# Delta-rule attention with a gated convolution behind it: the state kept as its block diagonal

## The chip, the cores and the metric

One core of a Trainium2 chip runs the kernel. The time is the device time in microseconds of one execution, from the launch of the program to its end; the smaller it is, the better. Beside it stands one execution taken by the hardware profiler, whose span runs from the first instruction to the last.

## What is computed

Four batches of eight heads, 768 tokens, 40 values a head. A state of 40 x 40 per batch and head is carried over the tokens; then 320 values a token go through a gated layer with a convolution over three tokens.

```python
for t in range(S):
    y[:, :, t] = einsum('bhd,bhde->bhe', r_t, state)
    Sa = einsum('bhde,bhe->bhd', state, a_t)
    state = state * w_t[:, :, None, :] - einsum('bhd,bhe->bhde', Sa, b_t)
    state = state + einsum('bhd,bhe->bhde', v_t, k_t)
x = y.transpose(0, 2, 1, 3).reshape(B, S, H * D)        # 4 x 768 x 320
h = maximum(x @ w_in, 0)                                 # 320 -> 1024
gate = sigmoid(conv over t of h with conv_w, three taps)
out = (h * gate) @ w_out                                 # 1024 -> 320
```

The weights of the second part come as 64-bit floats, all else as 32-bit floats.

## The kernel before

**Tiling.** The tokens are cut into 24 steps of 32. The four batches stand beside one another, 32 tokens each, on 128 partitions (`quad(bi)` is the batch's quarter). Two steps make a pair j for loading and solving, and also a window of 64 tokens for the second part. Heads are taken in three groups g of 120 values (three heads), at columns `GC = (0, 120, 200)`, so the third group overlaps the second by one head.

**The parts of a step** (two letters each in the written order):

- `ld` loads w, a, k, b of a pair; `lr` and `lv` load r and v of a step, one transfer a batch. `de` makes the products of w before and behind each token (`pre`, `suf`) with VectorE scans, and `wc`, the decay over a whole step, one column for each head with zeros elsewhere. `dd` turns a, k, b on TensorE and multiplies by these products (`ah`, `kt`, `bt`).
- `sc` makes three masked copies of `ah` (`ap`, ScalarE) and with them the 32 x 32 scores `at`; `si` and `so` solve the triangular system of a pair on VectorE (even j) or GpSimd (odd j), with the scores sent through DRAM before and the result after. `ha` turns k and b back to `khat`, `bhat`, with tokens on partitions.
- `ch` is the recurrence, in four parts. First `pp` = a times the old state (line 514) plus the scores times v (522), copied to `psb` by ScalarE. Then `pu` = solve times `psb` (533), copied to `u`. Then `pn` = khat times v plus bhat times u (549): for every batch and group a full 120 x 120 block, of which the three 40 x 40 blocks on the diagonal are the states. VectorE adds `pn` to the old state (562), 120 x 360 for each batch. Last, GpSimd multiplies by `wc` (568), which also clears what lies off the diagonal.
- `rt`, `vt`, `ut` turn r, v, u; r also in three masked copies `rp` (579) beside the plain one `rt` (584). `st` turns the state, three transposes and one ScalarE copy `sn` for each batch (602, 604). `pa` and `ou` make the step's result `py` from the turned state (629) and the masked pairs (638); `fi` turns and scales it into `xf` and splits it into a rounded part `xh` and the rest `xl`.
- `pk` packs with three transfers the rows that the second part's last passes need; `mi` does x @ w_in (eight passes, line 700), the convolution, the sigmoid and the gate for two of eight column blocks; `mo` the product with w_out (754) and the store. `we` converts the 64-bit weights piece by piece on VectorE, ScalarE and GpSimd.

**Order.** Every part is a generator that yields between its stages. The string `ORDER` lists the parts one stage at a time, as all engines are to be given their instructions; `put` names what each stage needs done ahead of it, and `advance` runs that first where the order hasn't. Each engine works through its own list in that order; all transfers go through SP's queue. PSUM has eight banks: six for the attention (`bank`), two for the second part. `BUFS` gives the number of buffers of each name.

## Time and profile before

| | |
|---|---|
| median of three timed runs | 707.8 us (705.96 to 711.5) |
| the profiled execution, first to last instruction | 704.2 us |
| around the span, against the median of the runs | 3.6 us |
| mean granted TensorE clock | 0.903 |
| instructions | 29851 |
| TensorE matmul / weight load busy | 559.1 / 496.7 us |
| VectorE, ScalarE, GpSimd busy | 521.5, 360.5, 354.1 us |
| DMA | 53.40 MB in 242402 packets, 229000 of them under 512 B |

How to read it: PE is TensorE's matmul, PEld its weight load, which runs beside the matmuls; DVE is VectorE, ACT ScalarE, POOL GpSimd, SP the engine that issues the transfers. In a row for a group of instructions, `pn<-v,khat 32*120 32x120` means that `pn` is written from `v` and `khat`, with 32 rows and 120 columns of weights, and 32 partitions of 120 elements moving through; `xcount` is the number of records, then come busy time, mean ns of one, and the idle time of the engine before them with what ended it. The busy time of a group counts overlapping instructions once. A row of a timeline gives start, length, engine, line and instruction. The ends of matmuls are modelled, so the distance from one start to the next is the safer measure.

### The profile page before, as it was taken

The numbers are of one execution on the slowest core, as the hardware profiler recorded it, in microseconds if no ns is written. First come the engines' busy times: TensorE is split into PE (matmuls) and PEld (weight loads), VectorE is DVE, ScalarE is ACT, GpSimd is POOL, SyncE is SP. The second block draws the span as 40 slices with busy tenths as digits, with TensorE's granted clock in tenths as the row PEclk, the third lists the DMA queues.
The fourth block names the chain that finished last, engine by engine and source line by source line (L and its number), as shares of the span: only waits on it lengthen the run. The fifth ranks groups of instructions, "written<-read, shape, count | busy, mean of one in ns | idle before, by whom it ended". The sixth has DMA issues, their size and how long they took to land. (4 is left out here: it accounts for less than half of the span.)

```text
span 704.2 us, 29851 instructions
## 1 busy us (share of the span) xinstructions
PE 559.1 (79%) x13021; PEld 496.7 (71%) x13021; DVE 521.5 (74%) x1169; ACT 360.5 (51%) x884; POOL 354.1 (50%) x582
## 2 busy tenths in 40 slices
PE   4436765678688987988987996899998977899886
PEld 3335654666577876977867885788887876788775
DVE  6699789998988895558884478986869892446561
ACT  3322344354275455655464664477665545566661
POOL 2002884037785236783244883237976048854321
PEclk9756766897899998999999998999999999999998
DMA  8766456348036325444414356524444025021000
GB/s 139 121 117 117 96 111 103 86 103 159 7 61 107 61 49 90 87 78 81 84 29 90 75 95 101 81 61 68 86 69 87 11 65 84 20 50 32 22 29 19
DMA packets 242402, 53.40 MB, mean 76 GB/s; under 512 B 229000, under 2 KB 238112, under 8 KB 242272
## 3 DMA queue, kind: packets, MB, share of 16 engines
q1 hardware_dynamic: 242272, 51.50, 40.2%
q8 instruction: 102, 1.67, 1.0%
q14 instruction: 28, 0.23, 0.1%
HBM read 38.63 MB, written 10.22 MB: 69 GB/s over the span
## 5 line engine op out<-in xcount | busy, mean ns | idle before, releaser
L729 DVE SCALAR_TENSOR_TENSOR cc<-hb,cw,cc 128x256 f32<-128x256 f32 x192 | 107.0, 580 | 28.6 <-ACT cc L721 25.0
L568 POOL TENSOR_TENSOR s<-s,wc 120x360 f32<-120x360 f32 x88 | 75.2, 885 | 66.6 <-DVE s L562 66.6
L480 POOL TENSOR_TENSOR st<-xx,bb 128x126 f32<-128x126 f32 (+22 forms) x186 | 81.0, 436 | 20.8 <-DMA bb<-bd 8.1
L486 POOL TENSOR_TENSOR xx<-xx,st 128x126 f32<-128x126 f32 (+22 forms) x186 | 81.8, 440 | 14.6
L700 PE MATMUL ph<-xh,wih 120*128 120x256 f32 x288 | 56.2, 304 | 12.0 <-ACT hb L714 12.0
L562 DVE TENSOR_TENSOR s<-pn,s 120x360 f32<-120x360 f32 x88 | 40.6, 523 | 28.7 <-PE pn L549 28.7
L736 DVE TENSOR_TENSOR cc<-cc,hb 128x512 f32<-128x512 f32 x48 | 40.9, 859 | 26.2 <-ACT cc L734 26.1
L480 DVE TENSOR_TENSOR st<-xx,bb 128x126 f32<-128x126 f32 (+22 forms) x186 | 53.7, 289 | 7.5 <-DMA bb<-bd 1.7
L486 DVE TENSOR_TENSOR xx<-xx,st 128x126 f32<-128x126 f32 (+22 forms) x186 | 54.4, 292 | 6.4
L700 PEld LDWEIGHTS ph<-xh,wih 120*128 120x128 f32 x288 | 41.4, 193 | 17.0 <-ACT hb L714 13.8
L734 ACT ACTIVATE cc<-cc 128x512 f32<-128x512 f32 x48 | 30.5, 637 | 40.8 <-DVE cc L729 40.8
L667 POOL TENSOR_TENSOR xl<-xf,xh 120x384 fp32r<-120x384 f32 x24 | 26.3, 1095 | 44.8 <-ACT xh L665 44.8
L721 ACT ACTIVATE cc<-hb,cw 128x256 f32<-128x256 f32 x96 | 43.8, 507 | 5.0 <-POOL g21l L743 2.4
L427 ACT ACTIVATE ap<-ah,hmask 120x384 f32<-120x384 f32 (+1 forms) x72 | 36.6, 577 | 18.3 <-DVE ah L391 9.7
L604 ACT COPY sn<-pt 120x360 f32<-120x360 f32 x92 | 39.0, 470 | 10.9 <-PE pt L602 10.4
L602 PE MATMUL pt<-ident,s 120*120 120x120 f32 x276 | 40.7, 281 | 4.0 <-DVE s L562 2.4
L714 ACT ACTIVATE hb<-ph 128x512 f32<-128x512 f32 x48 | 28.8, 601 | 22.3 <-PE ph L700 20.5
L579 ACT ACTIVATE rp<-pr,hmask 120x384 f32<-120x384 f32 x72 | 36.7, 585 | 4.7 <-PE pr L576 4.3
L700 PE MATMUL ph<-xl,wih 120*128 120x256 f32 x192 | 39.0, 285 | 0.0
L533 PE MATMUL pu<-psb,tt 32*32 32x40 f32 x1536 | 22.4, 210 | 18.8 <-ACT psb L527 16.1
L602 PEld LDWEIGHTS pt<-ident,s 120*120 120x120 f32 x276 | 31.6, 144 | 6.1 <-DVE s L562 2.8
L533 PEld LDWEIGHTS pu<-psb,tt 32*32 32x32 f32 x1536 | 18.6, 115 | 23.6 <-ACT psb L527 18.1
(867 smaller groups left out, 1661.8 us busy)
## 6 DMA issues: line engine op xcount, KB each, us to landing
bb<-bd SPq DMA_DIRECT2D x24, 256.0 KB
w<-in_w_dram SPq DMA_DIRECT2D x24, 160.0 KB
a<-in_a_dram SPq DMA_DIRECT2D x24, 160.0 KB
k<-in_k_dram SPq DMA_DIRECT2D x24, 160.0 KB
b<-in_b_dram SPq DMA_DIRECT2D x24, 160.0 KB
r<-in_r_dram SPq DMA_DIRECT2D x96, 40.0 KB
v<-in_v_dram SPq DMA_DIRECT2D x96, 40.0 KB
out_dram<-ob SPq DMA_DIRECT2D x22, 160.0 KB
```

Source lines behind the costliest of these rows:

```text
L480: eng.tensor_tensor(t3, xx[:, 0:nj, i : i + 1].to_broadcast([128, nj, nt]), bb[:, i : i + 1, i + 1 :].to_broadcast([128, nj, nt]), ALU.mult,)
L486: eng.tensor_tensor(xx[:, 0:nj, i + 1 :], xx[:, 0:nj, i + 1 :], t3, ALU.add)
L533: nc.tensor.matmul(pu[quad(bi), hc], tt[quad(bi), c, h, :], psb[quad(bi), hc], start=(h == 0), stop=True, skip_group_check=True,)
L562: nc.vector.tensor_tensor(new, pn[bi][:GR], old[bi], ALU.add)
L568: nc.gpsimd.tensor_tensor(n4, n4, w4, ALU.mult)
L579: nc.scalar.activation(out=rp[:, :, h, :], in_=pr[:GR], func=AF.Copy, scale=hmask[:, h : h + 1])
L602: nc.tensor.transpose(pt[:GR, g, :], old[bi][:, g, :], ident[:GR, :GR])
L604: nc.scalar.copy(sn, pt[:GR])
L700: nc.tensor.matmul(ph[:, j], l[:, fs], x, start=(j == 0 and i == 0), stop=(i == len(passes) - 1), skip_group_check=True,)
L721: nc.scalar.activation(out=cc[:, j], in_=hb[:, j, :, 1 : W + 1], func=AF.Copy, scale=cw[:, 1, f : f + 1],)
L729: nc.vector.scalar_tensor_tensor(out=cc[:, j], in0=hb[:, j, :, x : W + x], scalar=cw[:, x, f : f + 1], in1=cc[:, j], op0=ALU.mult, op1=ALU ...
L736: nc.vector.tensor_tensor(cc, cc, hb[:, :, :, 1 : W + 1], ALU.mult)
```

## The change

The state of a step becomes one tile of 120 x 480: for each batch and group the 120 rows (three heads of 40) and only 40 columns, that is the three diagonal blocks on top of one another. To write that form, `khat` and `bhat` are kept in 840 columns, each head's 40 among zeros (`slots`, `spot`), so that a window of 120 columns holds one head and zeros for the two others; `pn` then takes 32 products of 40 columns a side, which add up in place. `pp` and `py` read the state head by head, with the masked copies `ap` and `rp` as weights; the plain `rt` goes. `st` turns all four batches with four transposes and one copy. The decay `wc` needs no zeros any more and is written by the product that made `al`. GpSimd scales the state of all batches in one instruction.

The groups become (3, 3, 2) heads without overlap. r and v are stored by head number modulo three (`at(q)` gives a head's place), which needs the heads in another order: `reorder` copies r and v in four blocks of steps (`CUT`) from DRAM to DRAM, 24 transfers a block, and a step's load is then one transfer. Tiles that are read past their last head get a constant pad once (`padded`). In the second part, the pack is two transfers into `xh` and `xl` themselves in place of `xp`, and the passes are ordered anew. Buffers and needs follow. The order string is another one throughout. Cut to its core:

```diff
-    ld=4, r=2, v=2, hat=2, suf=2, pre=3, al=2, wc=3, at=3, ah=3, kt=2, ap=1, rp=1, bb=1, xx=1, stmp=1,
-    tt=2, rt=1, s=2, psb=1, u=2, vt=2, sn=4, ms=1, ysb=1, xf=2, xh=2, xl=2, xp=1, hb=2, cc=2, o=2,
+    r=2, v=2, hat=3, suf=2, pre=3, wc=3, at=3, ah=2, kt=2, ap=3, rp=1, bb=1, xx=1, stmp=1,
+    tt=2, s=2, psb=1, u=2, vt=2, sn=1, ms=1, xf=1, xh=2, xl=2, hb=2, cc=2, o=2,
...
-    ld0 de0.0*2 ld0*2 de0.1 ld0 ld1 de0.1 we0 dd0.0*3 dd0.1*2 sc0 dd0.1 we0 ld1*2 lr0 sc0 sc1 lr1
...
+    ld0*2 de0.0*2 de0.1*2 dd0.0 ld0 dd0.0 ld0 dd0.0 dd0.1 ld0 de0.0 de0.1 dd0.0 dd0.1*2 sc0 we0 we1
+    ld1 ha0 de1.0 ld1 we0*2 sc0 sc1 ha0 ha1 de1.0 ha0 de1.1 re0 ld1 we0 ha1 we0 we2 ld1 dd1.0 sc1
+    si0 sc1 ha1 we1 we2 dd0.1 ld1 we2 dd1.0 we1 re0 dd1.0 de1.1 re0 dd1.1*2 de1.1 re0 sc2 de1.0 lv0
+    lv1 dd1.1 so0*2 we2 so0 ld2 so0 we1 ha2 lv0 de2.0 vt0 so0*2 we3 lr0 so0*2 si0 we3 we4 sc2 ld2
+    we3*2 we5 de2.0 so0 we3 ch0 lr1 sc2 sc3 so0 rt0 sc3 lr0 so0 we4 so0 ch0 we4 we5 ch0*2 ut0 pa0
...
-GC = (0, 120, 200)
-GH = ((0, 3), (0, 3), (1, 3))
+NH = (3, 3, 2)
+CUT = (0, 2, 8, 16, 24)
+PG = 280
+PH = 120
...
+    def padded(name, at, value):
+        t = cp.tile([128, at + D], F32, name=name)
+        nc.gpsimd.memset(t[:, at:], value)
+        return t
+
+    inb = {nm: padded(f"in{nm}", 2 * HD, 1.0) for nm in "wakb"}
+    tok = {nm: [padded(f"{nm}{i}t", HD, 0.0) for i in range(BUFS[nm])] for nm in "rvu"}
+    ysb = padded("ysb", HD, 0.0)
+    hat = {}
+    for i in range(BUFS["hat"]):
+        for nm in "kb":
+            hat[nm, i] = cp.tile([128, G * PG], F32, name=f"hat{nm}{i}")
+            nc.vector.memset(hat[nm, i], 0.0)
...
-        nc.scalar.copy(wih[0:D, 2, :], wil[0:D, 2, :])
-        yield
-        nc.sync.dma_start(wil[2 * D : GR, 1, :].bitcast(F32), wil[D : 2 * D, 2, :].bitcast(F32))
-        nc.sync.dma_start(wil[0:D, 2, :].bitcast(F32), wil[2 * D : GR, 2, :].bitcast(F32))
-        nc.sync.dma_start(wil[D:GR, 2, :].bitcast(F32), wih[D:GR, 2, :].bitcast(F32))
+        for x, t in ((0, wih), (D, wil)):
+            nc.sync.dma_start(
+                t[2 * D : GR, 2, :].bitcast(F32), wil[x : x + D, 2, :].bitcast(F32)
+            )
+        yield
+        nc.scalar.copy(wil[0 : 2 * D, 2, :], wih[0 : 2 * D, 2, :].bitcast(F32))
...
+    def reorder(z):
+
+        t0, t1 = CUT[z] * C, CUT[z + 1] * C
+        for nm in "vr":
+            ordered[nm, z] = dc.tile([B, t1 - t0, HD], F32, name=f"{nm}o{z}")
         for bi in range(B):
-            nc.sync.dma_start(t[quad(bi)], x[bi, :, t0 : t0 + C, :].rearrange("h t d -> t h d"))
-        st[nm] = t.rearrange("p h d -> p (h d)")
+            for nm, x in (("v", v), ("r", r)):
+                for h in range(3):
+                    nc.sync.dma_start(
+                        ordered[nm, z][bi, :, 3 * h * D : (3 * h + NH[h]) * D].rearrange(
+                            "t (g d) -> t g d", d=D
+                        ),
+                        x[bi, h::3, t0:t1, :].rearrange("g t d -> t g d"),
+                    )
+            yield
+
+    def load(nm, st):
+        st[nm] = tok[nm][st["n"] % BUFS[nm]]
+        z = block(st["n"])
+        t0 = (st["n"] - CUT[z]) * C
+        nc.sync.dma_start(st[nm][:, :HD], ordered[nm, z][:, t0 : t0 + C, :])
...
-        al = buf(wn, [GR, NS, 1], "al", f"al{j}{y}")
-        nc.vector.tensor_tensor(al, suf[:, :, 0:1], wr[:, :, 1:2], ALU.mult)
-        nc.vector.reciprocal(dp0[:, :, 0:1], al)
+        al = pd["wc"].rearrange("p c (z y) g -> p y g z c", y=2)[:, y]
+        nc.vector.tensor_tensor(al, ends(suf, 0), ends(wr, 1), ALU.mult)
+        nc.vector.reciprocal(ends(dp0, 0), al)
         nc.vector.tensor_tensor_scan(
             out=flat(pd["pre"][:, y]), data0=flat(wr), data1=flat(dp0),
             initial=0.0, op0=ALU.mult, op1=ALU.add,
-        )
-        bc = [GR, 2 * G, 2, 3]
-        nc.vector.tensor_tensor(
-            pair(pd["wc"], y), al.rearrange("p (s c) x -> p s c x", c=2).to_broadcast(bc),
-            hmask.unsqueeze(1).unsqueeze(1).to_broadcast(bc), ALU.mult,
...
-            nc.scalar.copy(pd[nm][:, c], pz)
+            st[nm] = hat[nm, n % BUFS["hat"]]
+            nc.scalar.copy(
+                slots(st[nm]), pz.rearrange("p (g h d) -> p g h d", g=G, h=3)
+            )
             yield
 
+    def slots(t):
+
+        t = t.rearrange("p (g x) -> p g x", g=G)[:, :, : 2 * PH + D]
+        return bass.AP(tensor=t.tensor, offset=t.offset, ap=[*t.ap[:2], [PH, 3], [1, D]])
+
+    def spot(q):
+        return PG * (q // 3) + PH * (q % 3)
...
-            for g in range(G):
-                lo = GH[g][0] * D
+            for q, g, h in heads():
                 for bi in range(B):
                     nc.tensor.matmul(
-                        pp[quad(bi), GC[g] + lo : GC[g] + GR], ah[:, g, quad(bi)],
-                        old[bi][:, g, lo:],
-                        start=(g == 0), stop=False, skip_group_check=True,
+                        pp[quad(bi), q * D : (q + 1) * D], st["ap"][:, q, quad(bi)],
+                        old[:, bi, g],
...
-        for x, (l, m) in enumerate(((kk, vv), (bk, uu))):
-            for g in range(G):
+        pn = [bank([128, G, D], f"pn{n}{bi}") for bi in range(B)]
+        for x, (l, m) in enumerate(((st["k"], vv), (st["b"], uu))):
+            for q, g, h in heads():
+                lo = spot(q) - D * h
                 for bi in range(B):
                     nc.tensor.matmul(
-                        pn[bi][:GR, g, :], l[quad(bi), cols(g)], m[quad(bi), cols(g)],
-                        start=(x == 0 and g == 0), stop=(x == 1), skip_group_check=True,
+                        pn[bi][:GR, g, :], l[quad(bi), lo : lo + GR],
+                        m[quad(bi), at(q)],
+                        start=(x == 0 and q == 0), stop=(x == 1), skip_group_check=True,
                     )
+        new = state[n + 1] = buf(wn, [GR, B, G, D], "s", f"s{n}")
+        w4 = nxt["pd"]["wc"][:, nxt["c"]].unsqueeze(3).to_broadcast([GR, B, G, D])
         for bi in range(B):
-            new = wn.tile([GR, G, GR], F32, tag=f"s{bi}", bufs=BUFS["s"], name=f"s{n}{bi}")
-            n4 = new.rearrange("p g (h d) -> p g h d", h=3)
-            w4 = wc[:, :, bi, :].unsqueeze(3).to_broadcast([GR, G, 3, D])
             if first:
-                nc.vector.tensor_tensor(
-                    n4, pn[bi][:GR].rearrange("p g (h d) -> p g h d", h=3), w4, ALU.mult
-                )
+                nc.vector.tensor_tensor(new[:, bi], pn[bi][:GR], w4[:, bi], ALU.mult)
             else:
-                nc.vector.tensor_tensor(new, pn[bi][:GR], old[bi], ALU.add)
-            state[n + 1].append(new)
-            scaled.append((n4, w4))
+                nc.vector.tensor_tensor(new[:, bi], pn[bi][:GR], old[:, bi], ALU.add)
         yield
         if not first:
-            for n4, w4 in scaled:
-                nc.gpsimd.tensor_tensor(n4, n4, w4, ALU.mult)
-        yield
-
+            nc.gpsimd.tensor_tensor(new, new, w4, ALU.mult)
...
+    def at(q):
+
+        p = 3 * (q % 3) + q // 3
+        return slice(p * D, (p + 1) * D)
...
+        rp = st["rp"] = buf(wn, [GR, H, BC], "rp", f"rp{n}")
+        for g in range(G):
             nc.scalar.activation(
-                out=rp[:, :, h, :], in_=pr[:GR], func=AF.Copy, scale=hmask[:, h : h + 1]
-            )
-        if n:
-            st["rt"] = buf(wn, [GR, G, BC], "rt", f"rt{n}")
-            nc.scalar.copy(st["rt"], pr[:GR])
...
-        st["sn"] = []
+        pt = bank([128, B, GR], f"pt{n}")
         for bi in range(B):
-            pt = bank([128, G, GR], f"pt{n}{bi}")
-            for g in range(G):
-                nc.tensor.transpose(pt[:GR, g, :], old[bi][:, g, :], ident[:GR, :GR])
-            sn = buf(wn, [GR, G, GR], "sn", f"sn{n}{bi}")
-            nc.scalar.copy(sn, pt[:GR])
-            st["sn"].append(sn)
-            yield
+            nc.tensor.transpose(pt[:GR, bi, :], old[:, bi].rearrange("p g d -> p (g d)"), ident[:GR, :GR])
+        sn = st["sn"] = buf(wn, [GR, B, GR], "sn", f"sn{n}")
+        nc.scalar.copy(sn, pt[:GR])
...
-            for g in range(G):
-                lo = GH[g][0] * D
+            for q, g, h in heads():
                 for bi in range(B):
                     nc.tensor.matmul(
-                        py[quad(bi), GC[g] + lo : GC[g] + GR], st["rt"][:, g, quad(bi)],
-                        st["sn"][bi][:, g, lo:],
-                        start=(g == 0), stop=False, skip_group_check=True,
+                        py[quad(bi), q * D : (q + 1) * D], st["rp"][:, q, quad(bi)],
+                        st["sn"][:, bi, h * D : (h + 1) * D],
...
-        xp = wd["xp"] = buf(mo, [GR, B, W], "xp", f"xp{n}", F32R)
-        nc.sync.dma_start(xp[0 : 2 * D].bitcast(F32), xh[0 : 2 * D, 1].bitcast(F32))
-        nc.sync.dma_start(xp[2 * D : GR].bitcast(F32), xh[D : 2 * D, 2].bitcast(F32))
-        nc.sync.dma_start(xl[0:D, 2].bitcast(F32), xh[2 * D : GR, 2].bitcast(F32))
+        for x, t in ((0, xh), (D, xl)):
+            nc.sync.dma_start(t[2 * D : GR, 2].bitcast(F32), xh[x : x + D, 2].bitcast(F32))
...
-            (wil[:, 0], xh[:, 0]), (wih[:, 0], xl[:, 0]), (wih[:, 1], xl[:, 1]),
-            (wil[:, 1], xp), (wil[:, 2], xl[:, 2]),
+            (wil[:, 0], xh[:, 0]), (wil[:, 1], xh[:, 1]), (wih[:, 0], xl[:, 0]),
+            (wih[:, 1], xl[:, 1]), (wil[:, 2], xl[:, 2]),
...
-                (0, ("chain", 2 * (j - BUFS["ah"]) + 1), 1), (1, ("wakb", j), 3), (2, ("wakb", j), 4),
+                (0, ("scores", 2 * (j - BUFS["ah"]) + 1), 1), (1, ("wakb", j), 3), (2, ("wakb", j), 4),
...
+            (1, ("chain", 2 * (j - BUFS["at"]) + 1), 1), (0, ("chain", n - BUFS["ap"]), 1),
         )
         put(
             ("hats", n), lambda st=st: hats(st), (0, ("decayed", j, 1), 2), (1, ("decayed", j, 1), 3),
-            (0, ("hats", n - 1), 2), (0, ("outputs", 2 * (j - BUFS["hat"]) + 1), 1),
-            (0, ("chain", 2 * (j - BUFS["hat"]) + 1), 3),
-        )
-        put(
-            ("v", n), lambda st=st: load(v, "v", st), (0, ("v", n - 1), 1),
+            (0, ("hats", n - 1), 2), (0, ("outputs", n - BUFS["hat"]), 1),
+            (0, ("chain", n - BUFS["hat"]), 3),
...
+            ("v", n), lambda st=st: load("v", st), (0, ("reorder", block(n)), B), (0, ("v", n - 1), 1),
...
```

More of the change, by code (lines that the diff above doesn't have):

```diff
@@ L314, in cols, with heads @@
     def cols(g):
-        return slice(GC[g], GC[g] + GR)
+        return slice(g * GR, (g + 1) * GR)
+    def heads():
+        return ((q, q // 3, q % 3) for q in range(H))
     def load_wakb(pd):
@@ L576, in rturn @@
             nc.tensor.transpose(pr[:GR, g, :], st["r"][:, cols(g)], ident)
[L577 to L578 removed]
+        rp = st["rp"] = buf(wn, [GR, H, BC], "rp", f"rp{n}")
+        for g in range(G):
             nc.scalar.activation(
[L580 removed]
+                out=rp[:, by_rows(g)], in_=pr[:GR, : NH[g]], func=AF.Copy, scale=hmask[:, g : g + 1]
             )
[L582 to L584 removed]
         yield
@@ L654, in finish @@
         for g in range(G):
-            nc.tensor.transpose(pq[:GR, g, :], st["ysb"][:, cols(g)], ident)
+            nc.tensor.transpose(pq[:GR, g, :], ysb[:, cols(g)], ident)
         xf = buf(wn, [GR, G, B, C], "xf", f"xf{n}")
@@ L854, in tile_decay_delta_attention_then_conv_gate_moe @@
     )
+    for z in range(len(CUT) - 1):
+        put(("reorder", z), lambda z=z: reorder(z))
     for pd in pds:
@@ L899, in tile_decay_delta_attention_then_conv_gate_moe @@
         put(
-            ("r", n), lambda st=st: load(r, "r", st), (0, ("r", n - 1), 1),
+            ("r", n), lambda st=st: load("r", st), (0, ("reorder", block(n)), B), (0, ("r", n - 1), 1),
             (0, ("rturn", n - BUFS["r"]), 1),
```

253 lines of the change are left out of this document (139 added, 114 removed).

## The prediction

> **What bounds the kernel now.** I read the page's table of engines first, then the busy time in three stretches of the span (columns of the second: from and to, length, busy us and instructions of PE, PE's weight loads, DVE, ACT, POOL, then the granted clock, the DMA share and GB/s).
>
> ```profile
> span 704.2 us, 29851 instructions
> PE 559.1 (79%) x13021; PEld 496.7 (71%) x13021; DVE 521.5 (74%) x1169; ACT 360.5 (51%) x884; POOL 354.1 (50%) x582
> ```
> ```profile
> 0.00:200.00 200.00, 122.87 (x2921) 104.39 (x2921) 172.68 (x442) 74.30 (x176) 86.74 (x166) 0.77 0.54 102
> 200.00:650.00 450.00, 393.58 (x9503) 354.01 (x9501) 324.77 (x687) 259.57 (x643) 254.40 (x406) 0.96 0.40 71
> 650.00:704.30 54.30, 42.66 (x603) 38.31 (x601) 24.05 (x41) 26.62 (x66) 13.01 (x11) 0.94 0.07 23
> ```
>
> No engine bounds the whole. In the first 200 us VectorE is busy 172.7 us (86%), with the weight conversion and the first solves; TensorE has a clock of 0.77 there and much idle time. From 200 to 650 us TensorE is busy 393.6 of 450 us (87%) at a clock of 0.96, VectorE 72%. In the last 54 us TensorE leads alone. So the change has two prices: what it takes from VectorE counts early, what it does to TensorE counts after that. What is left of TensorE's idle time in the middle, 450 - 393.6 = 56.4 us, is made of waits, and I asked for them by releaser:
>
> ```profile
> engine line waited for: us in total, times, longest us
> PE ph L700 <- ACT hb L714: 11.2, 8, 5.4
> ...
> PE pu L533 <- ACT psb L527: 3.9, 5, 1.3
> PE pm L411 <- ACT rp L579: 3.9, 3, 3.3
> ...
> PE pn L549 <- ACT u L538: 2.6, 2, 1.6
> ```
>
> These four end with a ScalarE eviction and sum to 21.6 of the 56.4 us; the largest is the wait for hb, a copy out of a bank. No row of this answer waits for the state on GpSimd, so the recurrence itself is not what holds TensorE in this stretch.
>
> **The change on TensorE.** Three places issue other matmuls. Here are the blocks of one step, each to be read from its start to the start of the next row.
>
> ```profile
> 401.21 0.79 PE L533 MATMUL pu<-psb,tt 32*32 32x40 f32 x64
> 401.93 0.62 PE L700 MATMUL ph<-xh,wih 120*128 120x256 f32 x3
> ...
> 403.08 0.90 PE L549 MATMUL pn<-v,khat 32*120 32x120 f32 x24
> 403.80 0.81 PE L549 MATMUL pn<-u,bhat 32*120 32x120 f32 x24
> 404.54 0.53 PE L450 MATMUL pz15b<-ident,bt 120*128 120x120 f32 x3
> ...
> 410.24 1.67 PE L602 MATMUL pt<-ident,s 120*120 120x120 f32 x12 [1.59 <-ACT wx L366]
> 411.85 0.65 PE L411 MATMUL pm<-rp,vt 120*32 120x96 f32 x24
> ...
> 428.50 0.76 PE L514 MATMUL pp<-s,ah 120*32 120x120 f32 x24
> 429.19 0.79 PE L522 MATMUL pp<-v,at 32*32 32x40 f32 x64
> ```
>
> Each f32 matmul has two records, a transpose one. Four batches run side by side, so I speak of waves of four records.
>
> *sturn.* Twelve transposes of 120x120 become four, one bank and one copy in place of four. The twelve take 411.85 - 410.24 = 1.61 us; a third is 0.54. That is -1.07 us a step.
>
> *The state part of pp and py.* Twelve matmuls of up to 120 columns become 32 of 40 columns; the columns stay 320, the weight loads go from 24 records to 64. Now pp's 24 records take 429.19 - 428.50 = 0.69 us; 64 records of 40 columns take 0.72 in pu (401.93 - 401.21). pu has 32 rows and these have 120, so it is only the nearest row. Above, if each load held PE as the 24 do now, 64 x 0.69 / 24 = 1.84. I take 0.72: the 24-record blocks pm with 96 and 64 columns also run in pace with their columns. +0.03 twice a step, at most +1.15 each.
>
> *pn.* The doubtful one. Each of 12 products a side (120 weight columns, 120 moving) becomes 32 with the same 120 weight columns, of which 80 are zeros or padding, and 40 moving. Now both sides take 404.54 - 403.08 = 1.46 us, of which 12 waves at about 0.105 are 1.26 and 0.2 is the drain. After it there are 32 waves. If they ran as pu's, two blocks of 0.72 make 1.44: a change of nothing. If a wave cannot be shorter than the load of its 120 columns, they take 32 x 0.105 + 0.2 = 3.56: +2.10 a step. The trace has no wave with long loads and few moving columns, but it has the loads:
>
> ```profile
> L549 PEld LDWEIGHTS pn<-v,khat x552: 174/180/320, 61.8 to 636.1; 32*120 32x120 f32 x184
> ...
> L533 PEld LDWEIGHTS pu<-psb,tt x1536: 101/108/167, 60.6 to 646.7; 32*32 32x32 f32 x192
> ```
>
> A load of 120 columns lasts 180 ns and one of 32 columns 108, on the same 32 rows: 72 ns for 88 columns, 0.82 a column, so 98 ns of streaming for 120. A wave of 40 moving columns (0.72 / 16 = 45 ns, start included) doesn't hide that. I take the upper end, +2.10. The Trainium skill, "TensorE: Matmul & The Clock Gate", section "LDWEIGHTS (loading the stationary operand)", says the same against this change: a load costs columns / 1.2 ns, whatever the rows, so 32x120 costs an estimated 100 ns; by it the sum is the one taken here.
>
> A step then has -1.07 + 0.06 + 2.10 = +1.09 us of TensorE work. The middle has 17 such steps, as pn's records there show (816 of 48 a step):
>
> ```profile
> 200.00:650.00 450.00, 31.50 (x816) 27.31 (x816) 31.42 (x68) 0.96 0.40 71
> ```
>
> 17 x 1.09 = **+18.5 us** there. The first steps lie in the stretch that VectorE sets, and I count them as hidden; that cover gone, five steps would cost 5 us more.
>
> **The change on the other engines.**
>
> ```profile
> L568 POOL TENSOR_TENSOR s<-s,wc 120x360 f32<-120x360 f32 x88 | 75.2, 885 | 66.6 <-DVE s L562 66.6
> L562 DVE TENSOR_TENSOR s<-pn,s 120x360 f32<-120x360 f32 x88 | 40.6, 523 | 28.7 <-PE pn L549 28.7
> L604 ACT COPY sn<-pt 120x360 f32<-120x360 f32 x92 | 39.0, 470 | 10.9 <-PE pt L602 10.4
> L437 DVE TENSOR_TENSOR at<-ps,trin 128x512 f32<-128x512 f32 x24 | 16.4, 683 | 12.2 <-PE ps L411 10.2 <-DMA k<-in_k_dram 2.0
> L584 ACT COPY rt<-pr 120x384 f32<-120x384 f32 x23 | 11.4, 494 | 0.0
> L381 DVE TENSOR_TENSOR wc<-al,hmask 120x36 f32<-120x36 f32 x24 | 8.9, 371 | 0.0
> ```
>
> VectorE: 88 state additions shrink from 360 to 120 elements. From 523 (360) and 683 (512) an element costs 1.05 ns, so 120 cost about 271; between the 371 of the tiny wc and less, this is the value I take. 88 x 0.252 = 22 us less, and wc's product with the mask, 8.9, goes: -31 of 521.5. ScalarE: 92 copies of 470 become 23 of 480 elements, by the same reckoning (470 for 360, 494 for 384: 1.0 an element) 590: 43.2 - 13.6 = -30; rt's 11.4 goes; k-hat and b-hat grow from 320 to 360 elements, 48 x 0.04 = +1.9. About -40 of 360.5. GpSimd: 88 products of 885 become 23 of 480 elements, in proportion 1180: 77.9 - 27.1 = -51 of 354. From the last addition's start to a scaled state it was 4 x 0.523 + 4 x 0.885 = 5.6 us and is 2.3, which no wait in the middle asks for: worth nothing by itself.
>
> *Start.* The part of this that lies in the first 200 us:
>
> ```profile
> L562 DVE TENSOR_TENSOR s<-pn,s 120x360 f32<-120x360 f32 x20 | 9.2, 520 | 0.2 <-PE pn L549 0.2
> L381 DVE TENSOR_TENSOR wc<-al,hmask 120x36 f32<-120x36 f32 x10 | 2.6, 259 | 0.0
> ```
> ```profile
> 1.56 0.79 DVE L204 MEMSET wx<- 120x384 f32 x2
> 7.06 0.96 DVE L369 TENSOR_TENSOR_SCAN suf<-wx,dsuf 120x384 f32<-120x384 f32 x1 [3.25 <-ACT wx L365]
> ```
>
> 20 additions save 5 us and wc 2.6. Six new memsets of 840 columns cost, at 0.395 for 384, 0.86 each, 5.2 us; 3.25 of these fall into the wait ahead of the first scan. 7.6 - 1.9 = 5.7, and as VectorE is busy 86% of this stretch, **-5 us**. If the wait ahead of the scan moved too, it would be -3.
>
> *DMA and SP.* r and v came in eight issues a pair of tensors and step; now one each, but 24 issues a block (four blocks) reorder them first, DRAM to DRAM, in the same 160-byte pieces. Sums of issues: 192 become 48 + 96.
>
> ```profile
> 16.02 5.16 SPq L336 DMA_DIRECT2D r<-in_r_dram  x8
> ```
>
> At 5.16 / 8 = 0.65 us an issue, the first block is 24 x 0.65 = 15.5 us of SP's queue where the 16 issues of r and v for two steps were 10.3: +5 us in front of the next k, b and solve transfers queued behind. pn's first product, which reads v, runs only at 61.8 (its row above), behind the first solve; a load that follows a 15 us block issued in the first 30 us is there by then, so I cost it at nothing; without that cover it is 5. The pack loses one of three transfers, but now the third of eight passes, not the last two, needs it. With xp gone, SP no longer waits for xp's last reader, and the pack can go as soon as xl is written. Nothing, or up to 1 us in each of 12 windows.
>
> *Buffers.* k-hat and b-hat get three places of a step for two of a pair, ah two for three, xf one for two, ap three for one. xf's is the only new wait that can hold an engine: VectorE would stand for GpSimd's xl of the step before, with the next conversion or gate queued behind. Steps are 450 / 17 = 26 us apart, so nothing, and with two steps finished back to back one GpSimd pass each.
>
> *Order.* Read as a list, the new order puts the first chains, the middle and the last chain at the same shares of the list as the old (chain 12 at 0.49 in both, chain 22 at 0.90 and 0.89). More TensorE work lies between psb and its reader, but pairs now more often follows uturn at once, which waits for one ScalarE copy. I take no gain or loss from it, and 10 us either way for the range.
>
> **The sum.** What does the relief of ScalarE and VectorE give back in the middle? Below, a share of the waits equal to the work removed: ScalarE loses 11% (40 of 360.5), so 11% of 56.4 = 6 us. Above, the four ACT rows shown, 21.6, as if no eviction came late any more. I take 20, near the upper end: sn's copies come in runs of four in one queue with the evictions TensorE waits for, and sturn takes one bank where it took four. Middle: 18.5 - 20 = -1.5. Start -5. End (one sturn, one py) -1. Together -7.5; the span goes from 704.2 to 696.7. The profiled span lies 3.6 below the median of the runs shown (707.8), so **700 us**, 1.1% faster. About 1% is what a measurement of this kernel can tell from no change.
>
> **Rivals.**
>
> *The weight loads are hidden* (0.2). The next waves' loads run ahead far enough that pn stays at 1.44. Then 17 x 2.1 = 36 us less in the middle than in the forecast, of which I let 28 through, since other waits then show: 672. For it: four loads do run side by side now, within one wave of 105 ns. Against: 180 against 108 ns.
>
> *TensorE turns into the bound and the relief doesn't reach it* (0.3). The waits of TensorE that count are on hb, psb, u: each begins with TensorE's own result, and a shorter queue on ScalarE doesn't shorten that. Then the middle has 18.5 and gets 6 back, the lower end above, the first steps add 5 and the start gains nothing: 707.8 + 17.5 = 725; with the start's 5 gained, 720. I put 722. It decides when TensorE, at 87% now, is above about 92% in the middle.
>
> *The reorder holds up the start* (0.1). 15 us of SP, DRAM to DRAM, then a load that waits at the head of SP's queue for it, with the next b and bd behind: 5 us of issue and one more landing of some 3 us in each of the first two blocks: 707.8 + 8 = 716 with the rest at nought.
>
> *No load overlaps the matmul before it on its rows* (0.03, within the second). A wave of pn is then 98 + 45 = 143, 32 of them 4.6 us, +3.3 a step in place of 2.1, 20 us more: 719. Against it: now 98 of load and 105 of wave fit into 105. The same page, section "The mechanism", has this as a rule (loads overlap matmuls in flight only in other row groups); the trace of pn disagrees.
>
> **Numbers.** The forecast has 0.4, with a range of its own of 686 to 712. Chances: faster by over 1% (below 700.7): 0.2 from the hidden loads and 0.23 from the forecast: 0.43. Within: 0.14 from the forecast, 0.05 from the reorder and 0.07 from the milder second rival: 0.26. Slower: the rest, 0.31. The range of eight in ten reaches to just below the hidden loads, 669, and to the second rival with a little over it, 726.
>
> **What would show it.** pn's 128 records a step: a block of about 3.5 us confirms the load bound, 1.5 refutes it. pt: four records, one sn copy of 0.57. State additions of 0.27 and GpSimd products of 1.2. TensorE's busy share in the middle above 90% with the time unchanged speaks for the second rival. Weights busy (PEld) should rise by some 40 us if loads bound pn. SP waiting for a reorder ahead of the first v would show the third. I am wrong if the order itself moves the time by over 10 us, which nothing in the trace of before can tell.

## The result, and the profile after

The changed kernel takes **790.3 us** (median of four runs, 788.8 to 791.3) against 709.6 for the kernel before on the same chip: a ratio of 1.115, 95% interval 1.110 to 1.119. The forecast was 700 with a range up to 726. Ratios below are all against the kernel before and leave disturbed executions out (one of b_pn took 2944 us); some profiled executions were up to 2.3% above the best run of their kernel, so the spans of two traces compare only to that.

The head of the page, the row of the instruction queue from its third part, and the stretches (the middle now runs to 720):

```profile
span 789.3 us, 36523 instructions
PE 631.8 (80%) x16517; PEld 576.9 (73%) x16517; DVE 473.8 (60%) x1151; ACT 328.3 (42%) x792; POOL 291.4 (37%) x527
q8 instruction: 129, 2.11, 1.2%
```
```profile
0.00:200.00 200.00, 123.59 (x3271) 107.22 (x3272) 139.50 (x378) 52.96 (x121) 53.49 (x116) 0.68 0.56 103
200.00:720.00 520.00, 453.88 (x12273) 420.29 (x12273) 308.79 (x726) 242.68 (x592) 221.61 (x398) 0.88 0.39 74
720.00:789.30 69.30, 54.31 (x975) 49.41 (x973) 25.50 (x49) 32.64 (x80) 16.29 (x14) 0.94 0.06 17
```

VectorE, ScalarE and GpSimd lost 48, 32 and 63 us, where 31, 40 and 51 were forecast; TensorE's matmuls are 72.7 us busier, its clock in the middle fell from 0.96 to 0.88, and its idle time grew only from 145.1 to 157.5. What the idle time is made of changed. Its waits by releaser (line, releaser: us, times, longest):

```profile
PE py L709 <- issue: 20.0, 14, 2.8
PE pw L421 <- DMA inw<-in_w_dram: 16.9, 2, 16.1
...
PE pp L594 <- issue: 7.5, 3, 3.4
```

Summed over the whole answer, waits for ScalarE and VectorE fell from 106 to 56 us; those for transfers rose from 13 to 45 and those for "issue", in which nothing else in the profile holds the engine, from 14 to 43. The same view of before has py with less than half of it:

```profile
PE py L638 <- issue: 8.0, 8, 1.7
```

**What "issue" is here.** A stretch of TensorE's timeline in the changed kernel, with py of one step and pp of the next:

```profile
489.54 0.80 PE L700 MATMUL py<-sn,rp 120*32 120x40 f32 x64
490.27 0.47 PE L709 MATMUL py<-hatk,ms 32*32 32x40 f32 x27
492.39 0.52 PE L709 MATMUL py<-hatk,ms 32*32 32x40 f32 x35 [1.65 <-issue]
492.72 0.22 PE L709 MATMUL py<-hatb,ms 32*32 32x40 f32 x2
492.74 0.20 PE L709 MATMUL py<-hatk,ms 32*32 32x40 f32 x2
492.75 0.76 PE L709 MATMUL py<-hatb,ms 32*32 32x40 f32 x62
493.45 0.47 PE L594 MATMUL pp<-s,ap 120*32 120x40 f32 x26
497.34 0.89 PE L594 MATMUL pp<-s,ap 120*32 120x40 f32 x38 [3.42 <-issue]
```

Between the two stops lie some 128 matmul records (35 + 2 + 2 + 62 + 26 and the edge), that is 256 with their loads. Numbering all of TensorE's records through, matmuls, loads and its sequencer's, I find stops (over 0.3 us from one start to the next) at one and the same place in every 256: 33 of them, 53.3 us, against 18 and 18.4 us before. The instruction queue fits: 2.11 MB in 129 packets are 16 KB each, and 2 x 16517 records / 129 = 256; before it was 102 packets for 2 x 13021. TensorE's instructions come in packets of 256, and where short matmuls use one up in 1.5 us the next is not there. The Trainium skill, "Runtime: NRT & Kernel Launch", section "Instruction fetch mechanics", describes these blocks of 16 KiB and 256 instructions; that crossing one is "mostly hidden", as it says, is not so here: 53.3 us. I hadn't drawn on it in the forecast.

**The clock.** A block of pn at full and at half clock, each read to the start of the next row, and the granted clock (third figure from the end) over the two:

```profile
505.07 1.89 PE L627 MATMUL pn<-v1t,hatk 32*120 32x40 f32 x64
506.78 1.87 PE L627 MATMUL pn<-u1t,hatb 32*120 32x40 f32 x64
508.57 0.61 PE L521 MATMUL pz17b<-ident,bt 120*128 120x120 f32 x3
```
```profile
224.42 3.62 PE L627 MATMUL pn<-v1t,hatk 32*120 32x40 f32 x63
227.65 0.41 PE L627 MATMUL pn<-u1t,hatb 32*120 32x40 f32 x3
227.85 0.40 PE L627 MATMUL pn<-v1t,hatk 32*120 32x40 f32 x1
227.85 3.59 PE L627 MATMUL pn<-u1t,hatb 32*120 32x40 f32 x61
231.37 0.90 PE L421 MATMUL pb<-ident,inb 128*120 128x128 f32 x3
```
```profile
224.40:231.40 7.00, 6.98 (x128) 6.87 (x128) 0.30 (x2) 0.50 0.06 15
505.00:508.60 3.60, 3.52 (x128) 3.45 (x128) 0.00 (x0) 1.00 0.08 7
```

3.50 us at full clock, as forecast (3.56), and 6.95 at half. From span and mean clock, half-clock time is 2 x (1 - clock) x span, as the clock stands at 0.5 or 1 in the records: with 0.903 it was 2 x 0.097 x 704.2 = 137 us before, with 0.835 it is 2 x 0.165 x 789.3 = 260 after.

### The profile page after: what moved, and what is told of

Read it like the earlier page. It is cut to its first block, busy times and chain, and to the rows that moved or that the text cites. A ratio compares the mean times of both kernels' runs of the same rounds, so it can differ in the third digit from the quotient of the medians.

```text
span 789.3 us, 36523 instructions
## 1 busy us (share of the span) xinstructions
PE 631.8 (80%) x16517; PEld 576.9 (73%) x16517; DVE 473.8 (60%) x1151; ACT 328.3 (42%) x792; POOL 291.4 (37%) x527
## 3 DMA queue, kind: packets, MB, share of 16 engines
q8 instruction: 129, 2.11, 1.2%
## 4 chain that ended last, share of the span: by engine, by line
PE 55%; DVE 15%; issue 8%; DMA 7%; ACT 7%; POOL 6%; SPq 1%; DVEq 0%; POOLq 0%; ACTq 0%
PE pn L627 12%; PE po L822 9%; PE ph L768 7%; PE pm L479 4%; PE py L709 4%; DMA xd<-xx 3%; DVE xx L567 2%; DVE st L561 2%; PE pu L613 2%; POOL xx L567 2%; POOL st L561 2%; PE ps L479 2%; PE pp L602 2%; DMA xh<-xh 2%; PE py L700 2%
## 5 line engine op out<-in xcount | busy, mean ns | idle before, releaser
L797 DVE SCALAR_TENSOR_TENSOR cc<-hb,cw,cc 128x256 f32<-128x256 f32 x192 | 98.7, 536 | 46.7 <-ACT cc L789 43.3
L561 POOL TENSOR_TENSOR st<-xx,bb 128x126 f32<-128x126 f32 (+22 forms) x186 | 75.6, 407 | 21.5 <-DMA bb<-bd 8.5
L641 POOL TENSOR_TENSOR s<-s,wc 120x480 f32<-120x480 f32 x22 | 23.1, 1049 | 145.3 <-DVE s L638 145.3
L768 PE MATMUL ph<-xh,wih 120*128 120x256 f32 x288 | 62.6, 327 | 13.6 <-ACT hb L782 7.2
L638 DVE TENSOR_TENSOR s<-pn,s 120x120 f32<-120x120 f32 x88 | 18.8, 274 | 68.6 <-PE pn L627 68.4
L768 PEld LDWEIGHTS ph<-xh,wih 120*128 120x128 f32 x288 | 46.5, 213 | 16.8 <-ACT hb L782 8.0
L782 ACT ACTIVATE hb<-ph 128x512 f32<-128x512 f32 x48 | 28.7, 599 | 44.6 <-PE ph L768 41.0
L686 DVE TENSOR_TENSOR ms<-pm,tri 128x512 f32<-128x512 f32 x24 | 16.5, 689 | 45.2 <-PE pm L479 45.1
L768 PE MATMUL ph<-xh,wil 120*128 120x256 f32 x192 | 42.4, 306 | 0.4 <-issue 0.4
L714 ACT COPY ysb<-py 128x320 f32<-128x320 f32 x24 | 10.2, 425 | 69.1 <-PE py L709 69.1
L657 ACT ACTIVATE rp<-pr,hmask 120x384 f32<-120x384 f32 (+1 forms) x72 | 33.9, 543 | 3.6 <-PE pr L654 3.3
```

Of the source, the lines that this page charges most:

```text
L561: eng.tensor_tensor(t3, xx[:, 0:nj, i : i + 1].to_broadcast([128, nj, nt]), bb[:, i : i + 1, i + 1 :].to_broadcast([128, nj, nt]), ALU.mult,)
L657: nc.scalar.activation(out=rp[:, by_rows(g)], in_=pr[:GR, : NH[g]], func=AF.Copy, scale=hmask[:, g : g + 1])
L768: nc.tensor.matmul(ph[:, j], l[:, fs], x, start=(j == 0 and i == 0), stop=(i == len(passes) - 1), skip_group_check=True,)
L797: nc.vector.scalar_tensor_tensor(out=cc[:, j], in0=hb[:, j, :, x : W + x], scalar=cw[:, x, f : f + 1], in1=cc[:, j], op0=ALU.mult, op1=ALU ...
```

## The experiments

All against the kernel before (half-clock time and stops at packet edges from each one's trace):

| kernel | median us | ratio (95%) | half clock, us | stops, us |
|---|---|---|---|---|
| changed | 790.3 | 1.115 (1.110 to 1.119) | 260 | 53.3 |
| a_loads | 768.1 | one undisturbed run, 750 | 239 | 63.0 |
| a_few | 765.1 | one undisturbed run, 752 | 198 | 24.7 |
| a_both | 737.3 | 1.034 (1.022 to 1.046) | 182 | 42.0 |
| b_pn | 796.7 | 1.116 (1.102 to 1.130) | 246 | 28.7 |
| b_pp | 743.6 | 1.049 (1.043 to 1.055) | 171 | 53.3 |
| a_pass | 789.1 | 1.111 (1.102 to 1.120) | 249 | 51.7 |
| a_order | 938.7 | 1.325 (1.318 to 1.333) | 410 | 47.3 |
| a_pe | 705.2 | 0.987 (0.982 to 0.992) | 177 | 25.3 |
| a_pn12 | 736.5 | 1.038 (1.033 to 1.043) | 191 | 56.3 |
| a_mix | 807.7 | 1.130 (1.119 to 1.141) | 226 | 55.9 |
| b_reorder | 741.6 | 1.045 (1.042 to 1.049) | 171 | 20.3 |
| a_pe_noro | 684.0 | 0.959 (0.954 to 0.965) | 140 | 25.4 |
| a_noro | 784.7 | 1.103 (1.100 to 1.106) | 238 | 51.0 |
| b_spread | 716.1 | 1.008 (1.005 to 1.012) | 140 | 11.6 |

**Cutting the two suspects from the changed kernel.** `a_loads` loads 32 columns for pn where it loaded 120:

```
- pn[bi][:GR, g, :], l[quad(bi), lo : lo + GR],
+ pn[bi][:(GR if x == 0 and h == 0 else C), g, :],
+ l[quad(bi), lo : lo + (GR if x == 0 and h == 0 else C)],
```

> The changed kernel with short weight loads in pn: only the first product of each group and batch loads 120 columns, the others load 32 (the sums of the other rows are left out). Loads as the cause: pn's block falls from 3.5 to about 1.9 us, 23 x 1.6 = 37 us directly and more by the clock: 725 to 750 us. Instructions as the cause (TensorE runs out of fetched instructions): the same number of them in less time, so the stalls grow from 53 towards 70 us and the time stays at 780 to 800. Order or transfers as the cause: 750 to 760, the direct saving and nothing else.

`a_few` runs the state parts of pp and py as 12 matmuls in place of 32:

```
- for q, g, h in heads():
-   pp[quad(bi), q * D : (q + 1) * D], st["ap"][:, q, quad(bi)], old[:, bi, g]
+ for g in range(G):
+   pp[quad(bi), g * GR : g * GR + NH[g] * D], st["ap"][:, 3 * g, quad(bi)], old[:, bi]...[:, : NH[g] * D]
(the same for py)
```

> The changed kernel with the state products of pp and py issued as 12 of 120 columns in place of 32 of 40 (the same columns, 80 matmul and load records fewer per place and step; the head masks are left out of them). Instructions as the cause: the stalls fall from 53 to about 25 us and the clock rises: 745 to 765 us. Loads as the cause: TensorE's block of pp changes by 0.04 us, so 785 to 790.

`a_both` makes both edits.

> Both edits of the two kernels before it at once. If loads and instructions are the whole cause: 700 to 715 us, the time of before or a little under it, since ScalarE, VectorE and GpSimd have less to do. If the order or the transfers have a part: 725 to 745.

Each alone gives back 22 to 40 us and both together, by the ratios, (1.115 - 1.034) x 708 = 57 of the 81. a_few came out as its first reading had it; a_loads, by its median, fell between its readings: the stops grew to 63 us as the second said, but the time fell as well. 24 us were still open after a_both, in the range that I had put down to order or transfers.

**Adding each to the kernel before.** `b_pn` cuts each of pn's products into three of 40 moving columns with the 120 weight columns loaded again (144 records a step); `b_pp` cuts the state parts of pp and py in the same way (64 for 24). Both compute all of the reference.

```
  for g in range(G):
+   for h in range(3):
+     hd = slice(h * D, (h + 1) * D)
-     pn[bi][:GR, g, :], l[quad(bi), cols(g)], m[quad(bi), cols(g)]
+     pn[bi][:GR, g, hd], l[quad(bi), cols(g)], m[quad(bi), cols(g)][:, hd]
```

> The kernel before with pn's products cut into three of 40 moving columns, each with the same 120 weight columns loaded again; all else as it was. Loads as the cause: pn's two blocks go from 1.46 to about 3.9 us, 23 x 2.4 = 56 us, and the clock is at half speed for 50 us longer or more: 770 to 790 us. Loads hidden: 707 to 715. Instructions as the cause: 192 more a step, but spread over a slow block, so at most 10 us: 715.

```
- pp[quad(bi), GC[g] + lo : GC[g] + GR], ah[:, g, quad(bi)], old[bi][:, g, lo:]
+ for h in range(GH[g][0], 3): lo = h * D
+   pp[quad(bi), GC[g] + lo : GC[g] + lo + D], ah[:, g, quad(bi)], old[bi][:, g, lo : lo + D]
```

> The kernel before with the state products of pp and py cut into pieces of 40 columns (80 more records and as many loads a step and place, no more columns, all else as it was). Instructions as the cause: TensorE's stalls at the end of a fetched packet grow from 18 to 40 us or more, and with the clock that follows them the time is 735 to 750 us. If the fetch keeps up: 708 to 713, 0.04 us for each of 46 blocks and little else.

b_pp, which adds short records and no columns, takes 35 us more; its stops rise by 35 (18.4 to 53.3), and 22.1 us of its waits are issue ahead of py. That the two figures agree is chance in part: between the traces TensorE's idle time grows by 19 us (164.5 for 145.1) and its busy time by 19 (578.0 for 559.1), with 34 us more at half clock. So the stops cost by themselves, and the half clock beside them costs about as much: in 34 us of it TensorE loses 17 us of work. b_pn's 82 us come with 109 us more at half clock and 10 us more of stops; 708 + 82 is the upper end of what I expected of the loads.

```profile
PE py L640 <- issue: 22.1, 17, 3.0
```

**The two mechanisms by themselves.** `b_probe` appends four stretches to the kernel before, each of four batches side by side on 32 rows: loaded and moving columns 120/40, 120/120, 32/40, 32/120. Its own time means nothing.

> The kernel before with four stretches of products put behind its end, whose results nobody reads: 120 columns loaded and 40 moving; 120 and 120; 32 and 40; 32 and 120. If waves that wait for loads count as idle for the clock, the first stretch has a wave about every 105 ns and a granted clock near 0.5 with no gap on TensorE, the second the same pace at 1.0. If only gaps pull the clock down, both have 1.0. The third asks for 256 instructions in 1.44 us: a fetch that keeps up gives 0.72 us for 64 records, one that doesn't gives stalls of 1 us or more at each packet of 256. The fourth is the control: 1.0 and no stalls.

Busy time of its records in a window of each stretch (columns as above; clock third from the end):

```profile
705.00:754.00 49.00, 49.00 (x988) 49.00 (x984) 0.00 (x0) 0.00 (x0) 0.00 (x0) 0.50 0.01 3
760.00:786.00 26.00, 25.38 (x935) 24.63 (x932) 0.00 (x0) 0.00 (x0) 0.00 (x0) 1.00 0.02 4
790.00:840.00 50.00, 29.02 (x1706) 26.85 (x1694) 0.00 (x0) 0.00 (x0) 0.00 (x0) 0.57 0.02 4
855.00:889.00 34.00, 32.40 (x1179) 30.90 (x1171) 0.00 (x0) 0.00 (x0) 0.00 (x0) 0.95 0.02 4
```

With 120 columns loaded for 40 that move, TensorE never stands still and yet gets half the clock for all 49 us (the stretch begins at 700.6 at the full clock, which falls at 704.5 with no gap before it); with the same loads and 120 moving it has the full one. With short loads and short matmuls it stands still 42% of the time: 1706 records in 50 us are 128, a packet, every 3.75 us. That isn't for want of clock: the first long stop, 2.9 us, ends at 795.07, and the clock falls only at 796.7; the packets are 4.0 us apart up to there and 3.5 to 4.0 behind it. The Trainium skill, "TensorE: Matmul & The Clock Gate", section "What's actually happening", ties the clock to how busy TensorE has lately been; busy as the trace counts it is not what decides here, since the 49 us are busy throughout. It may be something nearer to columns moved; what exactly, these runs don't tell.

**Not the order, not the pack.** `a_order` gives the changed kernel the old order string with the reorders put in; `a_pass` puts the passes that read packed rows last again.

> The changed kernel with the order string of before (the parts of the reorder put where the first loads need them). If the new order is what costs: 750 to 770 us. If it is neutral: 780 to 800. Loads and instructions are the same, so neither theory gives less than 770.

> The changed kernel with the passes of the second part put so that the two that read the packed rows come last, as before. TensorE waited 6 us for the pack, and the chain has more of it: 778 to 786 us if that wait costs what it lasts, 790 if other waits take its place.

The old order's 938.7 us lie far outside both readings. It was made for other buffers and needs than the changed kernel has, so this run can't say what the new order is worth by itself, and no other run does. The pack costs nothing that shows (789.1 for 790.3).

**All of TensorE's shapes put back.** `a_pe` is a_few with pn as 12 products of 120 loaded and 120 moving columns; `a_pn12` puts back pn alone.

```
- for q, g, h in heads(): ... pn[bi][:GR, g, :], l[quad(bi), lo : lo + GR], m[quad(bi), at(q)]
+ for g in range(G): ... pn[bi][:GR, g, :], l[quad(bi), PG * g : PG * g + GR], m[quad(bi), cols(g)]
- nc.vector.tensor_tensor(new[:, bi], pn[bi][:GR], old[:, bi], ALU.add)
+ nc.vector.tensor_tensor(new[:, bi], pn[bi][:GR, :, :D], old[:, bi], ALU.add)
```

> The changed kernel with TensorE's work in the state product and in the two state parts cut back to the size it had before the change: pn as 12 matmuls of 120 loaded and 120 moving columns into banks [120, 3, 160], of which the add and the decay read the first 40 columns of each group, and the state parts as 12 matmuls of 120 columns (what is left out: the right values of the state sums and the state parts). The relief of VectorE, ScalarE and GpSimd, the reorder and the new order stay. Theory A (the load-bound waves, their number of instructions, and the half clock and the instruction fetch that come with them are the whole cause): 690 to 710 us, half-clock time back to about 140 us, and stalls at the edge of an instruction packet back to about 18 us; at 690 the relief that was forecast would show. Rival B (the new order or the transfers, put for 30 us in the version with both cuts, which stood at 737 us): 725 to 740 us with TensorE's shapes of before.

> The changed kernel with pn alone cut back to the size it had before (12 matmuls of 120 loaded and 120 moving columns into banks [120, 3, 160], the add and the decay read the first 40 columns of each group; left out: the right values of the state sums); the state parts stay at 64 records each. With both cut back the kernel took 705 us, with neither 790. Theory A (the prices of the two parts stand side by side: the state parts' instructions cost 25 us where they were cut from the changed kernel and 35 us where they were added to the kernel before): 728 to 740 us. Rival B (only the load-bound pn costs; the state parts hurt only beside it): 703 to 715 us. Rival C (half the price is joint): 715 to 728 us.

The loss is gone in a_pe, though not all of the half clock (177 us, where I expected some 140). What a_both still had over it, (1.034 - 0.987) x 708 = 33 us, is then pn's too, since the two kernels differ in nothing else. TensorE's busy time in pn, in a_both and in a_pe:

```profile
0.00:738.00 738.00, 70.91 (x2944) 59.41 (x2944) 19.63 (x92) 0.88 0.43 81
```
```profile
0.00:707.50 707.50, 45.55 (x1104) 38.91 (x1104) 19.40 (x92) 0.87 0.45 84
```

a_both runs 128 records a step, 12 of the 64 products still with long loads, where a_pe runs 48: 25 us more; the stops are 42.0 us for 25.3. So what a_both left open was pn's, its remaining long loads and its many records together. What the transfers cost is still in both kernels (a_pe_noro, below). The steps between the ratios give the prices: state parts (1.038 - 0.987) x 708 = 36 us, with the stops going from 25 to 56; pn (1.115 - 1.038) x 708 = 54 us, with the stops unchanged and half-clock time from 191 to 260. b_pp gives the same 35; b_pn's 82 for 144 records has no such counterpart.

**Diluting pn.** `a_mix` keeps every instruction of the changed kernel and puts pieces of the second part, where ready, between pieces of 24 to 40 records of pn:

```
  (pn) for q, g, h in heads(): ... matmul ...
+        if q % 4 == 2: fill()     # next ready piece of mi or mo of the next 48 in the order
```

> The changed kernel, complete, with nothing altered but TensorE's order: pn's 128 records are cut into pieces of 24 to 40 wherever a piece of the second part (8 matmuls of 256 columns, or 6 of the output's) is ready in the next 48 parts of the order, which is so at some two places a step. The same matmuls, loads and instructions are run. Theory A (the half clock comes from a dense stretch of load-bound records, so that diluting it helps): half-clock time 262 to under 210 us, 750 to 775 us, slips of a step smaller. Rival B (the price is the records' own duration and the instruction fetch; the clock falls for other reasons): half-clock time above 240 us and 780 to 800 us. Rival C (the pieces put into pn hold up the state's chain): half-clock time down, but 790 us or more.

Half-clock time fell by 34 us and the kernel got 1 to 2% slower, as Rival C had it: TensorE's idle time is 173 us for 157.5. That it is the recurrence which pays for the pieces put in was not shown. Dilution helps the clock, but this way of it doesn't pay.

**The reorder.** In a_pe TensorE waits 44 us less than before for ScalarE and VectorE (62 for 106) and 52 us more for transfers (65 for 13):

```profile
PE pw L421 <- DMA inw<-in_w_dram: 19.6, 2, 15.1
...
PE pr L653 <- DMA r0t<-ro: 9.3, 2, 8.5
...
PE pvt L665 <- DMA v0t<-vo: 6.5, 1, 6.5
```

SP's queue in the changed kernel shows why (start, length, issues): 24 of the reorder stand ahead of the w of the third pair (the last row), which TensorE waits 16.1 us for. The expectation of a_noro below calls it the second.

```profile
9.08 1.32 SPq L378 DMA_DIRECT2D inw<-in_w_dram  x2
...
14.63 2.01 SPq L397 DMA_DIRECT2D vo<-in_v_dram  x3
16.69 1.90 SPq L397 DMA_DIRECT2D ro<-in_r_dram  x3
...
40.33 1.90 SPq L397 DMA_DIRECT2D ro<-in_r_dram  x3
42.40 0.63 SPq L409 DMA_DIRECT2D v0t<-vo  x1
43.06 0.56 SPq L409 DMA_DIRECT2D v1t<-vo  x1
43.67 1.68 SPq L378 DMA_DIRECT2D inw<-in_w_dram  x2
```

`b_reorder` gives the kernel before the reorder alone, placed by my hand:

```
- for bi in range(B): nc.sync.dma_start(t[quad(bi)], x[bi, :, t0 : t0 + C, :]...)
+ nc.sync.dma_start(st[nm], ordered[nm, z][:, t0 : t0 + C, :])     # after reorder(z), as in the change
```

> The kernel before with nothing of the change but the reorder of r and v in DRAM: 24 transfers a block in four blocks, then one load of r and one of v a step. Theory A (the reorder is harmless): 703 to 715 us, waits of TensorE for DMA up by under 6 us. Rival B (the reorder holds up the first steps or the work-window transfers behind it on SP's queue): 720 to 735 us, with the first steps late.

Rival B, and at 741.6 us above its range. The first solve's transfers on SP's queue, there and in the kernel before:

```profile
56.90 4.06 SPq L510 DMA_DIRECT2D xd<-xx  x2
66.45 1.72 SPq L515 DMA_DIRECT2D tt<-xd  x4
```
```profile
52.02 1.33 SPq L491 DMA_DIRECT2D xd<-xx  x2
55.67 1.71 SPq L496 DMA_DIRECT2D tt<-xd  x4
```

ScalarE's copy psb is 13 us late in the first step and 29 in the second, of 40 in the last: the loss arises at the start. It holds for that placement only; in the changed kernel the first psb comes at 56 us, before at 60.

`a_pe_noro` and `a_noro` take the reorder out of a_pe and of the changed kernel; r and v are read as before.

```
- nc.sync.dma_start(st[nm][:, :HD], ordered[nm, z][:, t0 : t0 + C, :])
+ for bi in range(B): nc.sync.dma_start(st[nm][quad(bi), :HD]..., x[bi, :, t0 : t0 + C, :]...)
```

> The version with TensorE's shapes of before (705 us, 0.987 of the kernel before), now also without the reorder: r and v are read straight from the inputs with four transfers a tensor and step, as before the change (left out besides the right state sums and state parts: the heads of r and v stand in another order than the rest expects). In that version TensorE's waits that end with ScalarE or VectorE are 62 us, against 106 before the change, but those that end with a transfer are 65, against 13. Theory A (the 24 transfers a block at the head of SP's queue, and the loads that wait for them, ate the relief): waits for transfers back under 35 us and 665 to 692 us. Rival B (the transfers are late for another reason, such as the order of the loads in the new string): 697 to 710 us.

> The changed kernel, TensorE's work as it is, without the reorder (r and v straight from the inputs, four transfers a tensor and step; the heads of r and v stand in another order than the rest expects). Theory A (the reorder costs what it holds up at the start): 765 to 782 us, with TensorE's wait for the second w of 16 us gone. Rival B (TensorE's own work covers it by the end, as its busy time sets this kernel): within 5 us of 790.

Without the reorder a_pe gains another (0.987 - 0.959) x 708 = 20 us, and its waits for transfers fall from 65 to 22 us. In the changed kernel it is worth (1.115 - 1.103) x 708 = 8, between the two readings: the waits for transfers fall from 45 to 21 us there, but those for ScalarE and VectorE rise from 56 to 82.

**Fewer short instructions in a row.** `b_spread` is the kernel before with py's products yielding in three parts, issued among the wide products of the second part.

> The kernel before with nothing changed but where the output products stand in TensorE's order: the 384 records of a step's outputs are cut into three parts, each issued among products of the second part with 512 columns, so that fewer instructions are run in one short time. Theory A (the instruction fetch, 18 us of stalls at the edges of packets in the kernel before, and the half clock behind some of them, is a price of many short instructions in a row): stalls 8 to 14 us, 695 to 703 us. Rival B (the later outputs hold up the state's chain, or the stalls move to the next run of short instructions): 707 to 720 us.

The stops fell to 11.6 us as expected, and the time rose by 0.8%: Rival B. TensorE's waits for transfers rose from 13 to 22 us; what holds it up wasn't followed further. So fewer stops brought no gain by themselves here. No complete version tried here beats the kernel before.

## Why the prediction was wrong

*What held.* pn is bound by its loads (3.50 us a block for 3.56). The step of the state turn, the additions, the scaling and the copy came out as forecast:

```profile
L641 POOL TENSOR_TENSOR s<-s,wc 120x480 f32<-120x480 f32 x22 | 23.1, 1049 | 145.3 <-DVE s L638 145.3
L638 DVE TENSOR_TENSOR s<-pn,s 120x120 f32<-120x120 f32 x88 | 18.8, 274 | 68.6 <-PE pn L627 68.4
L675 PE MATMUL pt<-ident,s 120*120 120x120 f32 x92 | 15.8, 299 | 2.2 <-issue 2.2
L677 ACT COPY sn<-pt 120x480 f32<-120x480 f32 x23 | 12.9, 560 | 8.6 <-PE pt L675 8.6
```

274 ns for 271, 560 for 590, 1049 for 1180. PEld rose by 80 us where 40 were the sign. Two signs that I had named for rivals did not come: TensorE's busy share of the middle stayed at 87% (453.9 of 520), and SP did not wait ahead of the first v, which it issues at 42.40, right behind the last reorder.

*Term by term, in us:*

| term | forecast | measured | from |
|---|---|---|---|
| state turn, relief, start, end | -44 (-18, -20, -5, -1) | -29 | a_pe_noro |
| reorder | 0 | +20, +8 in the finished change | a_pe against a_pe_noro; a_noro |
| state parts of pp, py | +1 | +36 | a_pn12 against a_pe; b_pp +35 |
| pn | +36 in the middle | +54 | changed against a_pn12 |
| sum | -7 | +81 | |

The measured steps lead from one version to the next, so they add up by construction. The first row holds all that a_pe_noro still has of the change, the new order, buffers and pack among it. Taken in another order the steps differ: the reorder is worth 8 us in the finished change, and the state parts, cut from it first (a_few), some 25 to 38.

1. **The state parts** are the step that failed. I costed 64 records in place of 24 by pu's pace, and by pace that was right: a block that the fetch leaves alone takes 0.73 us. But I priced each block alone and never asked how fast instructions arrive: b_pp's 35 us with 53.3 us of stops are the answer. The rows for it were there: q8's 102 packets and the waits of py for issue. Even my upper bound of 1.15 each, 39 us over 17 steps, was meant for another mechanism and never entered the range's upper end.
2. **pn** was mis-sized: right mechanism and duration, but I counted 17 of its 23 blocks and took those of the first 200 us as hidden behind VectorE. All 23 at +2.10 are 48 of the 54 us. The others did not stay hidden: the sixth step's copy psb starts 14 us later than in a_pn12, which has pn's old shape (a_pn12, then the changed kernel):

```profile
196.57 0.44 ACT L607 ACTIVATE psb<-pp 128x320 f32<-128x320 f32 x1 [2.39 <-PE pp L602]
```
```profile
210.44 0.44 ACT L607 ACTIVATE psb<-pp 128x320 f32<-128x320 f32 x1 [1.44 <-PE pp L602]
```

The rest fits the half clock that comes with it, 260 us for 191; the middle's 0.96 was used as if the change couldn't move it. TensorE's busy time in pn, in the same two kernels, grows by 58 us:

```profile
0.00:734.00 734.00, 46.99 (x1104) 40.09 (x1104) 19.41 (x92) 0.87 0.44 82
```
```profile
0.00:789.30 789.30, 104.72 (x2944) 100.65 (x2944) 19.61 (x92) 0.84 0.41 76
```

3. **The relief** was put at 20, near its upper end. TensorE's waits for ScalarE and VectorE did fall by 50 us in the change, but in a_pe_noro, with the transfers' waits down to 22 us, they are 91. TensorE is busy 26 us less there (533.3), which is the state turn's row, before and there:

```profile
L602 PE MATMUL pt<-ident,s 120*120 120x120 f32 x276 | 40.7, 281 | 4.0 <-DVE s L562 2.4 <-ACT wx L366 1.6
```
```profile
L667 PE MATMUL pt<-ident,s 120*120 120x120 f32 x92 | 14.4, 281 | 2.4 <-POOL s L633 2.4
```

It is idle 685.4 - 533.3 = 152 us against 145. So what shows of its gain is the state turn; no relief shows as less idle time. The two traces lie only 18.8 us apart, though, where the runs give 29, so up to 10 us of relief can't be ruled out. The second rival, that the relief doesn't reach TensorE, was right in the main. Whether the new order hid some of it wasn't tried. A slip beside it: with all 5.2 us of memsets on VectorE's path the start's gain would be 2 (86% of 7.6 - 5.2), not 3; nothing hangs on it.
4. **The reorder** was costed at nothing because v is needed late. What was late was, first of all, w, queued behind it, and then r and v too: in a_pe TensorE waits 19.6, 9.3 and 6.5 us for them; without the reorder w is at 8.7, and r0t and v0t have no wait. That is the third rival's place, with 24 us of wait by the longest rows of a_pe (15.1 + 8.5), where I had put 8.

The second rival's 722 erred like the forecast: it took TensorE to be bound by durations, with the clock and the supply of instructions fixed. The range was too narrow above for that reason.

## What to carry to other kernels

Count TensorE's instructions against its time as a resource of its own: in the probe's long run of short ones it got 128 matmuls with their loads per 3.75 us, and such a run stops at the next packet, which the page shows as "issue" and as packets of the instruction queue. A zero-padded weight that moves few columns is paid in its load and in the clock (a_pn12 against the changed kernel, +54 us), and a wide product cut into short ones is paid in instructions (b_pp, +35 us); compare columns loaded with columns moved, and count records, before trading wide products for exact ones. A block's cost is hidden only where it has been seen to be: pn's in the first steps wasn't. Before a transfer is called hidden, read what stands behind it on its queue.

## What the chip showed that I had not expected

TensorE at half clock while it never stands still: 49 us at 0.50 with 120 columns loaded for 40 moved, 1.00 with 120 moved. Loads of 120 columns into the same rows do overlap the matmuls before them (128 records in 3.50 us). And TensorE's instructions arrive in packets of 256, 16 KB each, one in 3.75 us on average in the probe's stretch of short matmuls, where it stood still 42% of the time.
